# Batch-wise transposes of the first chunk, early state products and later transposes of the second chunk in a fused attention and MLP kernel

## The chip, the cores and the metric

The kernel runs on one core of a Trainium2 chip. The metric is the device time of one execution in microseconds; lower is better. Each number of the profile comes from one profiled execution.

The engines are PE (TensorE: matrix products and transposes), DVE (VectorE), ACT (ScalarE), POOL (GpSimd, which here also issues the loads that change the type) and SP (SyncE, which issues the other DMAs).

## What is computed

Two steps, the second on the result of the first. The first is linear attention with decay, for 4 batches, 8 heads, 768 positions and a head size of 64, in blocks:

```python
for b in range(nb):
    ...
    intra = np.einsum('bhic,bhjc->bhij', qb, kb) * Dmask[None]
    intra = np.einsum('bhij,bhjd->bhid', intra, vb)
    inter = np.einsum('bhid,bhde->bhie', qb * lam_pow[None], kv_state)
    out[:, :, sl] = intra + inter
    kb_dec = kb * rev_pow[None]
    kv_state = lam_block[None, :, None, None] * kv_state + np.einsum('bhsd,bhse->bhde', kb_dec, vb)
```

The second is an MLP on the 3072 x 512 result x, with w_in (512 x 2048) and w_out (2048 x 512):

```python
h = x @ w_in
s = np.sin(alpha * h)
g = h + s * s / (alpha + 1e-09)
return (g @ w_out).astype(np.float32)
```

## The kernel before

**Tiling.** The 768 positions are cut into six chunks of 128 (`t` or `g`). A chunk of the four batches gives 512 rows of x, which are one group of the MLP. A unit `u = 4 t + b` is one chunk of one batch with all eight heads. Batch 1 of chunk 0 is u = 1, chunk 1 is u = 4 to 7.

**Attention of one unit.** `transposes(u)` (L173) makes QT and KT: eight transposes on PE into one PSUM tile of 128 x 1024, one copy on ACT (L183). `scores(u)` (L196) makes eight products F_ps on PE and the masked STm on DVE (L209). `intra_mm` and `inter_mm` (L244, L254) add STm times v and the state kv times QT in O_ps, and `copy_x(u)` (L261) scales O_ps by Etab into the tile xt of the chunk, on DVE. For chunk 0 there is no state yet, and `first_out` (L345) does the two steps without it.

**State.** `decay_k(u)` (L166) scales k on POOL into kdec. `state_mm(us)` (L213) makes 16 products a unit pair on PE and copies the result into kvs (for chunk 0 a plain copy on DVE, L227). `state_put` and `state_decay` on POOL bring it into kv and prepare the next sum.

**MLP of one group.** Sixteen steps f. `hidden(g, f)` (L278) is four products of 128 x 512 on PE into hps, then Sin on ACT (s_sb, L286) and the square s (L289), on ACT or, for even f up to 6 in group 0, on DVE (L295). `finish` (L292) makes gall on DVE, which also frees the PSUM buffer of hps. `project` (L305) multiplies four of the sixteen gall slices with w_out, and a copy on ACT and a DMA on SP follow the last of them.

**What sets the order.** The order of every engine is written out by hand: instructions stand on an engine in the order in which the code issues them, and an engine takes them strictly in that order. The parts that matter here:

- *Loads.* k and q of batch 0 come over SP as kraw and qraw and are cast on DVE (L334, L341). All else comes over POOL: chunk 0 for batches 1 to 3 (and v of batch 0), then the small identity idf (16 x 16, two POOL instructions, L125 and L126), then four parts of w_in, k and q of chunk 1 for batches 0 and 1, the last part of w_in, four `decay_k`, and the rest of chunk 1. A load on POOL waits until the eighth load before it has landed. The decayed k of chunk 0 comes behind all of w_in.
- *The front.* L362 to L402 lay out PE's order until the first `hidden(0, 0)`: for batch 0 KT and QT apart, in half tiles of 128 x 512 (L363 to L370), then batch after batch, with `spin(n)` between. `spin(n)` (L356) is n matmuls on a constant tile; nobody reads their result. The text calls them fills. Among them is `a_ps` (L387), a transpose of alpha with the identity idf; `alpha_sb` and `r_sb` (L392, L394) are made from it on DVE.
- *Group 0.* `slots(0)` (L426) says what PE does behind which step f. Behind f = 3 and 6 stand the state products of chunk 0 (`part_k`), behind f = 7 and 8 the transposes of units 4 and 5, behind f = 12 those of unit 6, behind f = 13 the products of unit 5 and the transposes of unit 7. `feed(0)` (L452) says what POOL does ahead of which step. At the end of group 0 (L503 to L512) the last two units of chunk 1 are finished between parts of `project(0, ...)`. `hidden(1, 0)` follows; it needs xt of all of chunk 1.

Of the kernel before, what the change touches and what calls it, by code (L numbers as in the profile page):

```python
# [9 lines left out]
ACTF = mybir.ActivationFunctionType  # L10
FP32 = mybir.dt.float32
# [4 lines left out]
def kernel(  # L16
# [11 lines left out]
    nc = tc.nc  # L28
    P = nc.NUM_PARTITIONS

    B, H, S, D = q.shape
# [13 lines left out]
    consts = ctx.enter_context(tc.tile_pool(name="consts", bufs=1))  # L45
# [25 lines left out]
    qn, kn, vn = {}, {}, {}  # L71
    KQV = ((kn, k), (qn, q), (vn, v))

    def new_chunk(t):
        for d, nm in ((qn, "qn"), (kn, "kn"), (vn, "vn")):
            d[t] = qkvp.tile([P, B, H, D], BF16, name=nm)
# [8 lines left out]
    def load(t, i, b0, b1):  # L85
        dst, src = KQV[i]
        nc.gpsimd.dma_start(  # L87
            out=dst[t][:, b0:b1, :, :].rearrange("p b h e -> p (b h) e"),
            in_=src[b0:b1, :, t * T:(t + 1) * T, :].rearrange("b h p e -> p (b h) e"))

    def load_w_in(i):
        f0, f1 = W_IN[i]
        nc.gpsimd.dma_start(out=w_in_sb[i][:],  # L93
                            in_=moe_w_in[:, f0 * P:f1 * P].rearrange("(c p) g -> p c g", p=P))
# [29 lines left out]
    load(0, 2, B - 1, B)  # L124
    idf = consts.tile([NFC, NFC], FP32, name="idf")  # L125
    make_identity(nc, idf[:])  # L126
    for i in range(4):
        load_w_in(i)
    new_chunk(1)
    load(1, 0, 0, 2)  # L130
    load(1, 1, 0, 2)
    load_w_in(4)

    kv = [consts.tile([P, HP, 2, D], BF16, name=f"kv{b}") for b in range(B)]
    for b in range(B):
# [30 lines left out]
    def decay_k(u):  # L166
        t, b = divmod(u, B)
        if t < NT - 1:
            kdec = kdp.tile([P, H, D], BF16, name="kdec")
            nc.gpsimd.tensor_tensor(out=kdec[:], in0=kn[t][:, b, :, :], in1=head_bc(Rtok), op=ALU.mult)  # L170
            st[u]["kdec"] = kdec

    def transposes(u, tag="pqk"):  # L173
        t, b = divmod(u, B)
        QK_ps = psA.tile([P, 2, HP, T], BF16, name="QK_ps", tag=tag)
        for hp in range(HP):
            nc.tensor.transpose(out=QK_ps[:, 1, hp, :],
                                in_=kn[t][:, b, 2 * hp:2 * hp + 2, :], identity=iden[:])
        for hp in range(HP):
            nc.tensor.transpose(out=QK_ps[:, 0, hp, :],  # L180
                                in_=qn[t][:, b, 2 * hp:2 * hp + 2, :], identity=iden[:])
        QKT = qkp.tile([P, 2, HP, T], BF16, name="QKT")
        nc.scalar.copy(out=QKT[:], in_=QK_ps[:])  # L183
        st[u]["QT"], st[u]["KT"] = QKT[:, 0, :, :], QKT[:, 1, :, :]
# [11 lines left out]
    def scores(u, halves=1):  # L196
        QT, KT = st[u]["QT"], st[u]["KT"]
        F_ps = psA.tile([P, 2, HP, T], FP32, name="F_ps", tag="pf")
        for hp in range(HP):
            for hd in range(2):  # L200
                nc.tensor.matmul(out=F_ps[:, hd, hp, :],  # L201
                                 lhsT=KT[hd * D:(hd + 1) * D, hp, :],
                                 rhs=QT[hd * D:(hd + 1) * D, hp, :],
                                 start=True, stop=True)
        STm = work.tile([P, 2, HP, T], BF16, name="STm")
        n = HP // halves
        for s in range(halves):
            w = slice(s * n, (s + 1) * n)
            nc.vector.tensor_tensor(out=STm[:, :, w, :], in0=F_ps[:, :, w, :], in1=Cmask[:, :, w, :],  # L209
                                    op=ALU.mult)  # L210
        st[u]["STm"] = STm

    def state_mm(us, tag="pqk"):  # L213
        KVA_ps = psA.tile([P, 2, HP, D], FP32, name="KVA_ps", tag=tag)
        for n, u in enumerate(us):
            t, b = divmod(u, B)
            for hp in range(HP):
                for hd in range(2):
                    h = 2 * hp + hd
                    nc.tensor.matmul(out=KVA_ps[hd * D:(hd + 1) * D, n, hp, :],  # L220
                                     lhsT=st[u]["kdec"][:, h, :], rhs=vn[t][:, b, h, :],
                                     start=True, stop=True)
        for n, u in enumerate(us):
            t, b = divmod(u, B)
            kvs[u] = ksp.tile([P, HP, D], FP32, name="kvs")
            if t == 0:
                nc.vector.tensor_copy(out=kvs[u][:], in_=KVA_ps[:, n, :, :])  # L227
            else:
                nc.vector.tensor_tensor(out=kvs[u][:], in0=KVA_ps[:, n, :, :], in1=kvd[b][:], op=ALU.add)  # L229

# [101 lines left out]


    nc.vector.tensor_copy(out=kn[0][:, 0, :, :], in_=kraw[:])  # L334
    for u in range(B):
        decay_k(u)
    load(1, 2, 0, 2)
    for i in range(3):
        load(1, i, 2, 4)
# [5 lines left out]
    def first_out(u, tag, hps_=range(4)):  # L345
        O_ps = psA.tile([P, HP, T], FP32, name="O_ps", tag=tag)
        for hp in hps_:
            for hd in range(2):
                nc.tensor.matmul(out=O_ps[hd * D:(hd + 1) * D, hp, :],
                                 lhsT=vn[0][:, u, 2 * hp + hd, :], rhs=st[u]["STm"][:, hd, hp, :],  # L350
                                 start=True, stop=True, skip_group_check=True)
        w = slice(hps_[0], hps_[-1] + 1)
        nc.vector.tensor_tensor(out=xt[0][:, w, u * T:(u + 1) * T], in0=O_ps[:, w, :],
                                in1=Etab[:, w, :], op=ALU.mult)

    def spin(n, cols=512):  # L356

        ps = psA.tile([P, GRP], FP32, name="hps", tag="h0")
        for _ in range(n):
            nc.tensor.matmul(out=ps[:, 0:cols], lhsT=fill[:, 0:P], rhs=fill[:, 0:cols], start=True, stop=True)  # L360

    spin(9)  # L362
    for nm, src, tag in (("KT", kn, "pqk"), ("QT", qn, "ops")):  # L363
        X_ps = psA.tile([P, HP, T], BF16, name="X_ps", tag=tag)
        for hp in range(HP):
            nc.tensor.transpose(out=X_ps[:, hp, :], in_=src[0][:, 0, 2 * hp:2 * hp + 2, :], identity=iden[:])
        XT = qkp.tile([P, HP, T], BF16, name=nm + "0")
        nc.scalar.copy(out=XT[:], in_=X_ps[:])
        st[0][nm] = XT[:]
        spin(3)  # L370
    scores(0)
    spin(1)
    transposes(1, "pqk")
    for hp in range(HP):
        nc.scalar.activation(out=Etab[:, hp, :], in_=pos_row[:], func=ACTF.Exp, scale=ln_hd[:, hp:hp + 1])
    spin(2)
    transposes(2, "ops")
    warm = consts.tile([P, 1], FP32, name="warm")
    nc.scalar.activation(out=warm[:], in_=lnlam[:, 0:1], func=ACTF.Sin)
    spin(1)  # L380
    scores(1)
    spin(1)
    first_out(0, "po")
    spin(1)
    scores(2)
    a_ps = psA.tile([P, NFC], FP32, name="a_ps", tag="h2")
    nc.tensor.transpose(out=a_ps[:], in_=alpha_fp[:], identity=idf[:])  # L387
    transposes(3, "pqk")
    spin(2)
    first_out(1, "h1")  # L390
    alpha_sb = consts.tile([P, NFC], FP32, name="alpha_sb")
    nc.vector.tensor_copy(out=alpha_sb[:], in_=a_ps[:])  # L392
    r_sb = consts.tile([P, NFC], FP32, name="r_sb")
    nc.vector.reciprocal(out=r_sb[:], in_=alpha_sb[:])  # L394
    spin(2)
    scores(3, 2)
    spin(1)
    first_out(2, "po")
    spin(2)
    first_out(3, "h1", range(0, 2))  # L400
    first_out(3, "ops", range(2, 4))
    spin(3)  # L402


    def part_fo(uf, uo, tag=None):
# [20 lines left out]
    def slots(g):  # L426

        u = [B * (g + 1) + b for b in range(B)]
        T_, FO = transposes, part_fo
        if g == 0:  # L430
            return {3: [(part_k, (0, 1), "pf")], 6: [(part_k, (2, 3), "pf")],
                    7: [(T_, u[0])], 8: [(T_, u[1], "po")], 9: [(FO, u[0], None)],
                    11: [(FO, u[1], u[0]), (copy_x, u[0])], 12: [(T_, u[2])],
                    13: [(FO, None, u[1]), (T_, u[3], "ops"), (copy_x, u[1])], 14: [(FO, u[2], None)]}, {}
        if g == 1:
            return {4: [(part_k, (4, 5), h_tag(1, 5))], 6: [(part_k, (6, 7), h_tag(1, 7))],
                    8: [(FO, u[0], None)], 10: [(FO, u[1], u[0], h_tag(1, 11))],
                    12: [(FO, u[2], u[1], h_tag(1, 13))],
                    14: [(FO, u[3], u[2], h_tag(1, 15)), (copy_x, u[2])],
                    15: [(FO, None, u[3], h_tag(2, 0)), (copy_x, u[3])]}, {10: u[0], 12: u[1]}  # L440
        at = (3, 6, 9, 12, 14) if g == 2 else (1, 4, 7, 10, 13)
        tg = [h_tag(g, f + 1) if g < NT - 2 else None for f in at[1:]]
        return {at[0]: [(FO, u[0], None)], at[1]: [(FO, u[1], u[0], tg[0])], at[2]: [(FO, u[2], u[1], tg[1])],
                at[3]: [(FO, u[3], u[2], tg[2])], at[4]: [(FO, None, u[3], tg[3])]}, \
               {at[n + 1]: u[n] for n in range(4)}
# [98 lines left out]
```

## Time and profile before

| | |
|---|---|
| median of 3 runs | 219.26 us (218.94 to 219.39) |
| profiled execution | 219.22 us, of which the span from the first to the last instruction is 217.5 us |
| PE | 208.3 us busy (96%) |
| ACT | 147.2 us (68%) |
| DVE | 126.6 us (58%) |
| POOL | 94.3 us (43%) |
| chain that ended last | PE 78%, POOL 10%, DMA 5% |
| first `hidden` of group 0 starts | 18.48 us |
| last ACT instruction of group 0 ends | 42.17 us |
| first `hidden` of group 1 starts | 46.26 us |

In timeline lines the columns are start, length, engine, line, operation, out<-in with shapes, and how many instructions were merged. In brackets stands how long the engine had been idle, and what ended that. A busy PE in this profile is not PE at its peak, since the ends of matmuls are modelled. The landing time of a load is its issue time plus the time to landing that the table of DMA issues gives.

### The profile page before, as it was taken

Reading aid. Unit: us, or ns where it says so; the run is one execution under the profiler, and the core shown is the slowest. Engines: PE = TensorE matmul, PEld = TensorE weight load, DVE = VectorE, ACT = ScalarE, POOL = GpSimd, SP = SyncE. Lnnn points to the kernel's source line nnn. Section 1 sums busy time; section 2 is a strip of 40 time slices with the busy share of each in tenths; the row PEclk is TensorE's granted clock in tenths of the full one; section 3 lists DMA queues with packets and bytes.
Section 4 is the critical chain, followed back from the end, with each engine's and each line's share of the span. In section 5 each row is a group of like instructions: output and inputs, shape, how many; then the busy total and the mean of one; then the engine's idle time right before and its main releaser. Section 6 shows DMA issues by size and latency. Waiting matters only on the chain.

```text
span 217.5 us, 3864 instructions
## 1 busy us (share of the span) xinstructions
PE 208.3 (96%) x1504; PEld 99.6 (46%) x1504; DVE 126.6 (58%) x183; ACT 147.2 (68%) x234; POOL 94.3 (43%) x131
## 2 busy tenths in 40 slices
PE   7799986999999999999999999999999999999994
PEld 2354443544444544445454444444444444444453
DVE  4576977834656875567656777545767544444300
ACT  5573998728766648766667675777676779787521
POOL 7999999963899569052474611100000000000000
PEclk9999999999999999999999999999999999999999
DMA  5999999999999999929689990490110101111022
GB/s 102 150 158 198 176 167 184 208 175 154 197 176 136 177 148 139 189 46 135 143 101 124 166 119 29 116 128 21 75 50 3 48 0 48 51 50 48 0 101 96
DMA packets 99747, 24.65 MB, mean 113 GB/s; under 512 B 91904, under 2 KB 96784, under 8 KB 99728
## 3 DMA queue, kind: packets, MB, share of 16 engines
q0 software_dynamic: 76976, 13.37, 79.0%
q1 hardware_dynamic: 22752, 11.03, 23.6%
q8 instruction: 12, 0.20, 0.4%
q14 instruction: 7, 0.06, 0.1%
HBM read 27.28 MB, written 6.29 MB: 154 GB/s over the span
## 4 chain that ended last, share of the span: by engine, by line
PE 78%; POOL 10%; DMA 5%; ACT 2%; issue 2%; DVE 1%; POOLq 0%; ACTq 0%
PE ops L311 36%; PE hps L283 32%; DMA qn<-in_q_dram 5%; PE O_ps L257 3%; PE F_ps L201 2%; POOL vn L87 2%; PE O_ps L249 2%; POOL kdec L170 2%; POOL qn L87 2%; POOL w_in L93 2%; PE KVA_ps L220 2%; PE hps L325 2%; POOL kn L87 2%; ACT s_sb L286 1%; ACT s L289 1%
## 5 line engine op out<-in xcount | busy, mean ns | idle before, releaser
L296 DVE SCALAR_TENSOR_TENSOR gall<-s,r_sb,hps 128x512 bf16<-128x512 bf16 x96 | 71.2, 745 | 67.0 <-ACT s L289 66.7
L286 ACT ACTIVATE s_sb<-hps,alpha_sb 128x512 bf16<-128x512 f32 x96 | 65.8, 687 | 49.7 <-PE hps L283 49.7
L283 PE MATMUL hps<-xt,w_in 128*128 128x512 bf16 x384 | 97.6, 379 | 0.1
L311 PE MATMUL ops<-w_out,gall 128*128 128x512 bf16 x368 | 93.0, 379 | 0.0
L289 ACT ACTIVATE s<-s_sb 128x512 bf16<-128x512 bf16 x92 | 58.0, 630 | 3.0
L283 PEld LDWEIGHTS <-w_in 128*128 128x128 bf16 x384 | 36.9, 98 | 44.3 <-DVE kvs L229 0.9
L311 PEld LDWEIGHTS <-gall 128*128 128x128 bf16 x368 | 34.8, 98 | 38.3
L235 POOL CAST kv<-kvs 64x256 bf16<-64x256 f32 x40 | 16.0, 401 | 41.8 <-PE O_ps L257 36.8
L209 DVE TENSOR_TENSOR STm<-F_ps,Cmask 128x1024 bf16<-128x1024 f32 (+1 forms) x25 | 29.4, 1178 | 3.8 <-PE F_ps L201 3.1
L170 POOL TENSOR_TENSOR kdec<-kn,Rtok 128x512 bf16<-128x512 bf16 x20 | 20.9, 1065 | 2.8 <-DMA kn<-in_k_dram 2.5
L316 ACT COPY o_sb<-ops 128x512 f32<-128x512 f32 x23 | 13.2, 572 | 6.4 <-PE ops L311 6.4
L263 DVE TENSOR_TENSOR xt<-O_ps,Etab 128x512 bf16<-128x512 f32 x20 | 13.7, 684 | 1.7 <-PE O_ps L257 1.6
L87 POOL DMA_DIRECT2D vn<-in_v_dram x12 | 14.2, 1195 | 0.0
L87 POOL DMA_DIRECT2D kn<-in_k_dram x11 | 13.5, 1227 | 0.3 <-issue 0.3
L87 POOL DMA_DIRECT2D qn<-in_q_dram x11 | 13.3, 1206 | 0.0
L360 PE MATMUL hps<-fill 128*128 128x512 bf16 x31 | 10.8, 455 | 1.5 <-DVE fill L112 1.5
L241 POOL TENSOR_TENSOR kvd<-kvs,L 128x256 f32<-128x256 f32 x16 | 9.8, 615 | 1.0
L249 PE MATMUL O_ps<-STm,vn 128*64 128x128 bf16 x160 | 8.0, 222 | 1.1 <-DVE STm L209 0.6
L183 ACT COPY QKT<-QK_ps 128x1024 bf16<-128x1024 bf16 x7 | 7.0, 1002 | 2.0 <-PE QK_ps L180 1.9
L249 PEld LDWEIGHTS <-vn 128*64 128x64 bf16 x160 | 5.3, 110 | 4.5 <-issue 3.5
L220 PEld LDWEIGHTS <-kdec 128*64 128x64 bf16 x160 | 3.8, 111 | 6.8 <-issue 6.4
L201 PE MATMUL F_ps<-QT,KT 64*128 64x128 bf16 x136 | 6.8, 219 | 0.0
(61 smaller groups left out, 84.5 us busy)
## 6 DMA issues: line engine op xcount, KB each, us to landing
out_dram<-o_sb SPq DMA_DIRECT2D x23, 256.0 KB, 2.7
w_out<-in_moe_w_out_dram POOLq DMA_DIRECT2D x4, 512.0 KB, 14.0
w_in<-in_moe_w_in_dram POOLq DMA_DIRECT2D x3, 512.0 KB, 9.5
kn<-in_k_dram POOLq DMA_DIRECT2D x6, 256.0 KB, 10.9
qn<-in_q_dram POOLq DMA_DIRECT2D x6, 256.0 KB, 11.3
vn<-in_v_dram POOLq DMA_DIRECT2D x6, 256.0 KB, 11.3
kn<-in_k_dram POOLq DMA_DIRECT2D x2, 512.0 KB, 7.5
qn<-in_q_dram POOLq DMA_DIRECT2D x2, 512.0 KB, 8.5
```

The lines of the kernel that those rows point to most:

```text
L87: nc.gpsimd.dma_start(out=dst[t][:, b0:b1, :, :].rearrange("p b h e -> p (b h) e"), in_=src[b0:b1, :, t * T:(t + 1) * T, :].rearrange("b h ...
L170: nc.gpsimd.tensor_tensor(out=kdec[:], in0=kn[t][:, b, :, :], in1=head_bc(Rtok), op=ALU.mult)
L209: nc.vector.tensor_tensor(out=STm[:, :, w, :], in0=F_ps[:, :, w, :], in1=Cmask[:, :, w, :], op=ALU.mult)
L235: nc.gpsimd.tensor_copy(out=kv[b][s, :, hd, :], in_=kvs[u][s, :, :])
L249: nc.tensor.matmul(out=O_ps[hd * D:(hd + 1) * D, hp, :], lhsT=vn[t][:, b, 2 * hp + hd, :], rhs=st[u]["STm"][:, hd, hp, :], start=(hp == 0) ...
L263: nc.vector.tensor_tensor(out=xt[t][:, :, b * T:(b + 1) * T], in0=st[u]["O_ps"][:], in1=Etab[:], op=ALU.mult)
L283: nc.tensor.matmul(out=hps[:], lhsT=w_in_of[f][:, c, :], rhs=xt[g][:, c, :], start=(c == 0), stop=(c == NDC - 1))
L286: nc.scalar.activation(out=s_sb[:], in_=hps[:], func=ACTF.Sin, scale=alpha_sb[:, f:f + 1])
L289: nc.scalar.activation(out=s2[:], in_=s_sb[:], func=ACTF.Square)
L296: nc.vector.scalar_tensor_tensor(out=gall[g][:, f, :], in0=s2[:], scalar=r_sb[:, f:f + 1], in1=hps[:], op0=ALU.mult, op1=ALU.add)
L311: nc.tensor.matmul(out=ops[:], lhsT=gall[g][:, f, m * P:(m + 1) * P], rhs=w_out_sb[part][:, f % 4, :], start=(f == 0), stop=(f == NFC - 1))
L316: nc.scalar.copy(out=o_sb[:], in_=ops[:])
```

## The change

Five edits, all of them moves or splits; no product of the computation is added or left out.

- *POOL.* Only the first two parts of w_in are loaded ahead of the decays. `decay_k(0)` and `decay_k(1)` come next, then a part of w_in, `decay_k(2)` and `decay_k(3)`, and the remaining loads in their old order.
- *Transposes of chunk 0.* `half_T` makes KT or QT of one unit by itself: four transposes and a copy of 128 x 512. Units 0, 1 and 3 go through it, unit 2 keeps the whole `transposes`.
- *Order of the front.* PE's order is laid out anew. `a_ps` stands behind the transposes of unit 1 (it stood behind scores(2)), `scores(1)` and all that follows behind it. `first_out(1)` stands ahead of `scores(2)`. There are 28 fills where there were 31.
- *States of chunk 0.* The two `state_mm` stand in the front, ahead of `hidden(0, 0)`, and not behind f = 3 and 6. Their copies into kvs move from DVE to ACT.
- *Group 0.* The transposes of unit 6 move from behind f = 12 to behind f = 13 and the products of unit 5, next to those of unit 7. (The `copy_x` of unit 5 is issued ahead of them.)

```diff
-    for i in range(4):
-        load_w_in(i)
-    new_chunk(1)
-    load(1, 0, 0, 2)
-    load(1, 1, 0, 2)
-    load_w_in(4)
+    load_w_in(0)
+    load_w_in(1)
...
             if t == 0:
-                nc.vector.tensor_copy(out=kvs[u][:], in_=KVA_ps[:, n, :, :])
+                nc.scalar.copy(out=kvs[u][:], in_=KVA_ps[:, n, :, :])
...
-    for u in range(B):
-        decay_k(u)
+    decay_k(0)
+    decay_k(1)
+    load_w_in(2)
+    decay_k(2)
+    decay_k(3)
+    load_w_in(3)
+    new_chunk(1)
+    load(1, 0, 0, 2)
+    load(1, 1, 0, 2)
+    load_w_in(4)
     load(1, 2, 0, 2)
...
+    def half_T(u, nm, tag):
+        src = {"KT": kn, "QT": qn}[nm]
         X_ps = psA.tile([P, HP, T], BF16, name="X_ps", tag=tag)
         for hp in range(HP):
+            nc.tensor.transpose(out=X_ps[:, hp, :], in_=src[0][:, u, 2 * hp:2 * hp + 2, :], identity=iden[:])
         XT = qkp.tile([P, HP, T], BF16, name=nm + "0")
         nc.scalar.copy(out=XT[:], in_=X_ps[:])
+        st[u][nm] = XT[:]
```

The front in its new order, from the first fills to the first `hidden` (the activations of Etab and of the table warm-up are on ACT):

```python
    spin(9)
    half_T(0, "KT", "pqk")
    spin(3)
    half_T(0, "QT", "ops")
    spin(1)
    half_T(1, "KT", "pqk")
    spin(1)
    scores(0)
    half_T(1, "QT", "ops")
    ...
    nc.tensor.transpose(out=a_ps[:], in_=alpha_fp[:], identity=idf[:])
    ...
    spin(2)
    scores(1)
    spin(1)
    transposes(2, "pqk")
    ...
    spin(1)
    first_out(0, "po")
    spin(2)
    first_out(1, "h1")
    scores(2)
    half_T(3, "KT", "ops")
    spin(1)
    half_T(3, "QT", "pqk")
    spin(1)
    first_out(2, "po")
    scores(3, 2)
    state_mm((0, 1), "h2")
    spin(4)
    first_out(3, "h1", range(0, 2))
    first_out(3, "ops", range(2, 4))
    state_mm((2, 3), "pqk")
    spin(2)
```

And group 0:

```diff
-            return {3: [(part_k, (0, 1), "pf")], 6: [(part_k, (2, 3), "pf")],
-                    7: [(T_, u[0])], 8: [(T_, u[1], "po")], 9: [(FO, u[0], None)],
-                    11: [(FO, u[1], u[0]), (copy_x, u[0])], 12: [(T_, u[2])],
-                    13: [(FO, None, u[1]), (T_, u[3], "ops"), (copy_x, u[1])], 14: [(FO, u[2], None)]}, {}
+            return {7: [(T_, u[0])], 8: [(T_, u[1], "po")], 9: [(FO, u[0], None)],
+                    11: [(FO, u[1], u[0]), (copy_x, u[0])],
+                    13: [(FO, None, u[1]), (copy_x, u[1]), (T_, u[2]), (T_, u[3], "ops")],
+                    14: [(FO, u[2], None)]}, {}
```

## The prediction

> **What bounds the kernel now.** I read the busy time by stage first, because the page's shares (PE 96%, ACT 68%) mix stages with different limits. The columns are the stretch, its length, then for PE, PEld, DVE, ACT and POOL the busy time and the number of instructions, PEclk, DMA share, GB/s.
>
> ```profile
> 1.52:18.48 16.96, 15.28 (x128) 6.91 (x129) 11.30 (x22) 9.39 (x17) 16.78 (x24) 1.00 1.74 156
> 19.54:42.17 22.63, 20.36 (x194) 10.18 (x193) 18.66 (x28) 21.01 (x32) 22.13 (x28) 1.00 1.79 184
> 46.26:214.30 168.04, 167.99 (x1153) 80.22 (x1151) 92.80 (x128) 115.68 (x184) 49.75 (x69) 1.00 0.87 99
> ```
>
> From 46.26 us to the last matmul PE is busy 167.99 of 168.04 us. Nothing else limits that part, so whatever moves the first product of group 1 (46.26) moves the end by the same amount. In group 0 (19.54 to 42.17) ACT is busy 21.01 of 22.63 us, nearly as full as PE. Before 18.48 no engine of the path is full: that stage is a chain of hand-overs.
>
> Next, the timeline of ACT in group 0, to see where its idle time lies:
>
> ```profile
> 19.54 0.69 ACT L286 ACTIVATE s_sb<-hps,alpha_sb 128x512 bf16<-128x512 f32 x1 [4.20 <-PE hps L283]
> ...
> 26.54 0.69 ACT L286 ACTIVATE s_sb<-hps,alpha_sb 128x512 bf16<-128x512 f32 x1 [0.28 <-PE hps L283]
> ...
> 36.51 1.01 ACT L183 COPY QKT<-QK_ps 128x1024 bf16<-128x1024 bf16 x1 [0.61 <-PE QK_ps L180]
> ...
> 41.54 0.63 ACT L289 ACTIVATE s<-s_sb 128x512 bf16<-128x512 bf16 x1
> 47.33 0.69 ACT L286 ACTIVATE s_sb<-hps,alpha_sb 128x512 bf16<-128x512 f32 x1 [5.15 <-PE hps L283]
> ```
>
> The bracket is idle time before the instruction and who ended it. Between its first s_sb (19.54) and the end of the last s (42.17) ACT idles four times worth naming: 0.17 (at 20.41) and 0.18 (at 24.34), which the same timeline shows, 0.28 and 0.61 here. That is 1.24 us, so **ACT's own work with its pipeline gaps is 42.17 - 19.54 - 1.24 = 21.39 us**, and none of it is touched by the change. The 0.61 is the stall that the change aims at: PE waits for the late q of chunk 1 before its transposes.
>
> ```profile
> PE QK_ps L180 <- DMA qn<-in_q_dram: 1.2, 1, 1.2
> ```
>
> The chain of waits shows how ACT's end becomes PE's start: last s, last gall, then
>
> ```profile
> 42.87 1.22 DVE STm L209
> 44.09 0.61 DVE xt L263
> 44.70 0.04 issue
> 44.74 0.41 PE O_ps L249 x8
> ```
>
> and from there the last xt of chunk 1 and hidden(1,0) at 46.26. The program keeps this order after the change (DVE: gall 15, STm 7, xt 6, xt 7), so those 4.09 us stay.
>
> **The front.** Its timeline, PE, POOL and DVE in turn:
>
> ```profile
> 8.39 0.40 PE L201 MATMUL F_ps<-QT,KT 64*128 64x128 bf16 x8
> ...
> 11.46 0.40 PE L201 MATMUL F_ps<-QKT 64*128 64x128 bf16 x8
> ...
> 13.51 0.23 PE L387 MATMUL a_ps<-idf,alpha_fp 16*128 16x16 f32 x1
> ...
> 18.48 0.81 PE L283 MATMUL hps<-xt,w_in 128*128 128x512 bf16 x3
> ```
> ```profile
> 11.50 0.19 POOL masks.py:199 TENSOR_SCALAR_AFFINE_SELECT idf<-idf 16x16 f32<-16x16 f32 x1
> ```
> ```profile
> 11.90 1.23 DVE L209 TENSOR_TENSOR STm<-F_ps,Cmask 128x1024 bf16<-128x1024 f32 x1 [1.85 <-PE F_ps L201]
> ```
>
> The reader is to see that the small transpose of alpha (a_ps) needs idf, which POOL finishes only at 11.69, behind its ten loads of chunk 0. Before, PE comes to a_ps at 13.51 and doesn't notice. The change puts a_ps right behind the second transpose of batch 1, ahead of scores(1). POOL's order up to idf is the same, so **PE gets a new wait**, and everything of the front is queued behind it.
>
> **The front, step by step.** Unchanged up to the QT copy of batch 0 (7.75 to 8.34). kn of batch 1 landed at 1.44 + 5.8 = 7.2, so its transposes fit at 7.8 to 8.2 in the gap; scores(0) at 8.39 as before; qn of batch 1 landed at 2.48 + 5.7 = 8.2, its transposes run 8.7 to 9.1 (0.39 a group of four). PE then idles until 11.73: 2.6 us.
> - a_ps 0.17 to its successor; two fills to 12.35 (0.59 for two less 0.38 for one: 0.21 each); scores(1) 12.45 to 12.85, against 11.46. STm 1: 12.9 to 14.1.
> - One fill, transposes(2) 13.0 to 13.6, its copy 1.01 to 14.65, then the Sin table 1.28 and warm 0.20 to 16.15, and only then the two half copies of batch 3 (0.59 each) to 17.25.
> - first_out(1) waits for STm 1: 14.6 to 15.0; scores(2) to 15.35; DVE xt 0, xt 1 (0.68 each) to 15.75, STm 2 to 16.87.
> - first_out(2) 16.9 to 17.3, xt 2 17.4 to 18.05. It now stands ahead of STm 3 on DVE, so DVE idles 0.5 while PE works; scores(3) 17.3 to 17.7 (KT, QT ready 17.25).
> - STm 3 in halves 18.0 to 19.2; on PE state_mm(0,1) 0.44, four fills to 18.95, first_out(3) 19.0 and 19.25 to 19.55; last xt 20.1.
> - state_mm(2,3) 0.44 and two fills: **hidden(0,0) at 20.4 instead of 18.48: 1.9 us later.**
>
> Bounds: with DVE's pieces back to back behind STm 1, STm 3 ends at 18.6; half of first_out(3) 0.3, state_mm 0.44 and two fills 0.43 give 19.8 (1.3 later). With 0.05 more at each of eight hand-overs, 20.8 (2.3 later).
>
> **Group 0.** ACT starts 1.06 after hidden(0,0), as now: 21.46. Of the four gaps the first 0.17 stays; 0.18 and 0.28 (PE late by state_mm, 0.44 each at 22.02 and 25.09) go with the moved states; 0.61 goes, since qn landed at 24.34 + 11.7 = 36.04 and ACT comes to that copy only near 38.7 (its s of f 12 ended at 35.91, now 1.46 later, then s_sb and s of f 13, 1.32). ACT ends at 21.46 + 0.17 + 21.39 = 43.02, against 42.17. **Sum: 1.92 - 1.07 = +0.85 us**, through the same tail to hidden(1,0) at 47.1 and so to the end. The removed stall of PE (0.46 + 1.17) is worth only the 0.61 that ACT idled. Behind it another wait is near: hidden(0,13) and batch 5's products stand ahead of the transposes now, and the O_ps buffer that they need is freed by xt 4 at about 37.6 (s of f 10 at 33.43 + 1.46 = 34.9, then gall 0.75, STm 5 1.22, xt 4 0.68 on DVE); transposes(6) end near 38.65, just ahead of ACT. I put 0 to 0.2 there.
>
> **Edits at no cost, and their cover.** DVE loses four state copies of 0.42, ACT gets four of 0.37 (the row of the final 128x256 copies) at 18.1 to 20.7, in the stretch where it idled 4.20; they would cost only if hidden(0,0) came before 19.6. Splitting two copies into halves adds 2 x 0.59 - 1.01 = 0.16 each, in idle time too. POOL's four decays (4.29 together) move ahead of five loads: w_in of f 4 is issued at 15.35 instead of 13.22, f 8 at 18.2 instead of 13.96, kn of chunk 1 at 19.0 instead of 14.69, vn of chunk 1 at 22.15 instead of 21.98. The order of all loads is the same and the DMAs have a backlog (w_in of f 2 lands at 12.49 + 5.7 = 18.2, after f 4 is issued), so I cost it at 0; a dry queue could shift landings by at most some 0.3. f 4 is wanted at 20.4 + 4 x 0.86 = 23.9 and landed at 13.22 + 7.6 = 20.8, f 8 not before 28 and 13.96 + 9.5 = 23.5: covered. Decay 3 ends at 18.25, before state_mm(2,3) wants it at 19.45. SP's queue is untouched.
>
> **The clock.** PE's first nine fills are 0.43 apart, until 5.54, which is 4.0 us after the first; later ones are 0.21 apart. At the end the clock fell:
>
> ```profile
> 213.90:217.30 3.40, 0.35 (x4) 0.07 (x1) 0.00 (x0) 0.37 (x1) 0.00 (x0) 1.00 0.22 79
> 217.20:217.50 0.30, 0.00 (x0) 0.00 (x0) 0.00 (x0) 0.00 (x0) 0.00 (x0) 0.66 0.00 0
> ```
>
> PE was busy 0.35 of the 3.40 us before 217.3, then the clock was half (mean 0.66). A new idle stretch of 2.6 us leaves a stretch of that length up to 23% busy at the worst place, more where it falls otherwise: between the 11% that lost the clock and the 81% (2.75 of 3.41, from 5.67 to 9.08) that kept it. Cost: 0, or, if PE then needs 4.0 us at half speed again, at most 4.0 / 2 = 2.0, part of it in waits. I take 0, because 11% is the nearer row and 23% is twice that, and keep 1.5 as a case. The Trainium skill ("TensorE: Matmul & The Clock Gate", Part 1) says that the clock is halved after at least one idle window of about 3.4 us. By that rule 2.6 us of idling cost nothing and the sum stays +0.85; by a reading in which a thinly used window counts as idle it would be about +2.35.
>
> **Rivals.**
> 1. *The clock falls* in the new wait: hidden(0,0) near 21.9, 219.22 + 0.85 + 1.5 = 221.6. For: 23% is nearer to 11% than to 81%. Against: the stretch must lie just so. 18%.
> 2. *Faster:* PE catches up in the front's slack (it has 1.7 us of gaps there), and group 0 gives its 1.07 us. The earliest start is set by decay 3 (18.25) with state_mm(2,3) and two fills behind it: 19.05, 0.57 late, so 219.22 - 0.5 = 218.7. It decides where hidden(0,0) starts before 18.48 + 1.07 = 19.55. Against: STm 1 alone is 1.0 late, and DVE's order adds 0.5. 10%.
> 3. *It cancels:* hidden(0,0) near 19.6, or ACT has slack that I don't see: 219.3. 12%.
>
> **Numbers.** The forecast has 60%. The profiled execution took 219.22 us (span 217.5), within 0.04 of the median 219.26, so +0.85 gives 220.1. The range, 219.2 to 221.7, holds the forecast's bounds (+0.3 to +1.45), the cancelling case and most of the clock's; outside are the faster case and the worst of the clock. About 0.2%, or 0.44 us, is what a measurement of this kernel can tell from no change. Faster by more: 0.10; within: 0.15 (case 3 and the low end of the forecast); slower: 0.75.
>
> **What would show it.** In the profile after: a gap of 2.6 us on PE ahead of a_ps, ended by POOL idf; scores(1) near 12.45; hidden(0,0) near 20.4; no DMA wait ahead of transposes(6); ACT from 21.5 to 43.0 with less than 0.3 us idle; hidden(1,0) near 47.1. I am wrong if hidden(0,0) starts before 19.6, if ACT shows gaps in group 0, or if PEclk shows less than 9 in slices 3 and 4 (10.9 to 21.7 us).

## The result

The changed kernel took **221.61 us** (median of 11 runs, 220.09 to 222.74), the kernel before 219.26 (11 runs, 218.94 to 219.59): a ratio of 1.0108, 95% interval 1.0082 to 1.0133. It is slower, and its runs spread over 2.6 us where those of before spread over 0.65. The profiled execution happens to be one of the quickest: 220.11 us, span 218.4. So the profile shows only one part of the loss, and the spread holds the other.

**The profile after.** The timeline of PE in the front:

```profile
8.70 0.40 PE L372 MATMUL X_ps<-iden,qn 128*128 128x128 bf16 x4
11.71 0.23 PE L389 MATMUL a_ps<-idf,alpha_fp 16*128 16x16 f32 x1 [2.61 <-POOL idf masks.py:199]
...
12.41 0.40 PE L197 MATMUL F_ps<-QT,KT 64*128 64x128 bf16 x8
...
20.47 3.83 PE L279 MATMUL hps<-xt,w_in 128*128 128x512 bf16 x17
```

The new wait is there, 2.61 us, and hidden(0,0) starts at 20.47 instead of 18.48. The timeline of ACT in group 0:

```profile
21.53 0.69 ACT L282 ACTIVATE s_sb<-hps,alpha_sb 128x512 bf16<-128x512 f32 x1 [0.97 <-PE hps L279]
22.40 0.69 ACT L282 ACTIVATE s_sb<-hps,alpha_sb 128x512 bf16<-128x512 f32 x1 [0.18 <-PE hps L279]
...
42.32 0.63 ACT L285 ACTIVATE s<-s_sb 128x512 bf16<-128x512 bf16 x1
48.10 0.69 ACT L282 ACTIVATE s_sb<-hps,alpha_sb 128x512 bf16<-128x512 f32 x1 [5.15 <-PE hps L279]
```

The gaps of 0.18, 0.28 and 0.61 that the prediction aims at are gone (the 0.18 shown here is the first gap, 0.17 before, which was to stay). ACT starts 1.99 later (21.53 against 19.54), ends 0.78 later (42.95 against 42.17), and the end of the span is 0.9 later. Behind that PE is full again, as the busy times of the stage from hidden(1,0) on show (columns as in the prediction):

```profile
47.04:215.10 168.06, 166.90 (x1132) 80.24 (x1151) 92.93 (x128) 115.64 (x184) 49.49 (x69) 1.00 0.88 99
```

That is 0.9 of 2.35 us. The rest does not show in this execution, whose granted clock was 1.000. Each run also has its mean granted clock, and of the 11 only two have 1.000. These took 220.09 and 220.11, all others 221.18 or more, at clocks from 0.985 to 0.992.

### The profile page after: what moved, and what is told of

It is laid out like the page before. It is cut to its first block, busy times and chain, and to the rows that moved or that the text cites. A ratio compares the mean times of both kernels' runs of the same rounds, so it can differ in the third digit from the quotient of the medians.

```text
span 218.4 us, 3832 instructions
## 1 busy us (share of the span) xinstructions
PE 205.8 (94%) x1474; PEld 100.0 (46%) x1501; DVE 125.6 (58%) x179; ACT 148.3 (68%) x240; POOL 93.9 (43%) x131
## 4 chain that ended last, share of the span: by engine, by line
PE 79%; DVE 7%; ACT 6%; POOL 4%; issue 3%; ACTq 0%; POOLq 0%
PE ops L307 34%; PE hps L279 32%; DVE gall L292 3%; PE O_ps L253 3%; PE F_ps L197 3%; ACT s_sb L282 2%; PE O_ps L245 2%; DVE STm L205 2%; ACT s L285 2%; PE KVA_ps L216 2%; PE hps L321 2%; POOL vn L87 2%; POOL qn L87 1%; ACT QKT L179 1%; PE hps L365 1%
## 5 line engine op out<-in xcount | busy, mean ns | idle before, releaser
L279 PE MATMUL hps<-xt,w_in 128*128 128x512 bf16 x374 | 96.4, 379 | 0.8 <-DVE gall L292 0.2
L307 PE MATMUL ops<-w_out,gall 128*128 128x512 bf16 x353 | 90.8, 379 | 0.8
L205 DVE TENSOR_TENSOR STm<-F_ps,Cmask 128x1024 bf16<-128x1024 f32 (+1 forms) x25 | 29.4, 1180 | 2.6 <-PE F_ps L197 2.0
L365 PE MATMUL hps<-fill 128*128 128x512 bf16 x26 | 10.2, 491 | 1.6 <-DVE fill L112 1.5
L197 PE MATMUL F_ps<-QT,KT 64*128 64x128 bf16 x152 | 7.6, 219 | 0.0
L179 ACT COPY QKT<-QK_ps 128x1024 bf16<-128x1024 bf16 x5 | 4.9, 1005 | 2.8 <-PE QK_ps L176 2.7
L225 DVE TENSOR_TENSOR kvs<-KVA_ps,kvd 128x256 f32<-128x256 f32 x16 | 6.7, 422 | 0.1
```

The lines of the kernel that those rows point to most:

```text
L197: nc.tensor.matmul(out=F_ps[:, hd, hp, :], lhsT=KT[hd * D:(hd + 1) * D, hp, :], rhs=QT[hd * D:(hd + 1) * D, hp, :], start=True, stop=True)
L279: nc.tensor.matmul(out=hps[:], lhsT=w_in_of[f][:, c, :], rhs=xt[g][:, c, :], start=(c == 0), stop=(c == NDC - 1))
L307: nc.tensor.matmul(out=ops[:], lhsT=gall[g][:, f, m * P:(m + 1) * P], rhs=w_out_sb[part][:, f % 4, :], start=(f == 0), stop=(f == NFC - 1))
```

## The experiments

Two theories were put against each other. **The clock:** the rest of the loss is a fall of PE's clock behind the idle stretch ahead of a_ps. **The loads:** it is late landings, from POOL's new order. Ratios are to the kernel before, timed on the same chip as each experiment.

### 1. Fills in the wait

```diff
+    spin(12)
     a_ps = psA.tile([P, NFC], FP32, name="a_ps", tag="h2")
```

> The changed kernel with 12 more fills just ahead of a_ps (12 x 0.216 = 2.6 us), so that PE works while it has to wait for idf. The wait stays, the idle stretch goes. Theory (the clock falls behind the idle stretch in most executions): hidden(0,0) still near 20.4, all executions near 220.1 (219.8 to 220.4), the spread of the changed kernel (220.09 to 222.74) gone, clock 1.000 in every one. Rival (the spread comes from loads that land late, or from the order of the front): 221.6 and the same spread.

Measured: 220.49 us (12 runs, 220.08 to 221.39), ratio 1.006 (1.0039 to 1.008). In its profile the wait for idf is as long as before but filled, and hidden(0,0) starts at the same time:

```profile
11.70 0.23 PE L390 MATMUL a_ps<-idf,alpha_fp 16*128 16x16 f32 x1 [0.24 <-POOL idf masks.py:199]
...
20.47 2.75 PE L279 MATMUL hps<-xt,w_in 128*128 128x512 bf16 x12
```

No run had a clock below 0.998, and six of the twelve lie between 220.08 and 220.39. Work that nobody reads makes the kernel about 1.1 us quicker: the idle stretch was the cost, not only the wait. But the other six runs reach 221.39 at clocks of 0.998 to 1.000, so the expected end of the spread did not come. Late loads are the candidate for that rest; experiments 2, 4 and 5 bear on it.

### 2. The changed kernel again

Unchanged, to see its runs beside their clocks.

> The changed kernel once more, to see executions in which the clock fell. Theory: the time goes with the granted clock. Executions at 1.000 take 220.1, those with one stretch of half clock of about 3.4 us (mean clock 0.992) about 221.6, those with two (0.985) about 222.6; hidden(0,0) near 20.4 in the first and 22 to 23 in the others. Rival: late loads make the spread; then time and clock are not ordered alike.

Measured: 221.65 us (6 runs, 220.11 to 222.87), ratio 1.0106 (1.0072 to 1.0141). With the 11 runs above, by mean clock:

| mean clock | runs | us |
|---|---|---|
| 0.999 to 1.000 | 4 | 220.09, 220.11, 220.11, 220.87 |
| 0.989 to 0.992 | 8 | 221.18 to 221.83 |
| 0.985 | 5 | 222.49 to 222.87 |

Time goes with the clock from row to row: 1.1 to 1.7 us for the first step, some 1.0 for the second. (Not within a row: the two runs at 0.989, 221.18 and 221.19, are quicker than those at 0.992.) One stretch of 3.4 us at half clock in a span of 219.9 gives 1 - 0.5 x 3.4 / 219.9 = 0.992, two give 0.985. Thirteen of 17 runs lost the clock; of the 96 runs of the kernel before, timed here and beside the experiments, three have a clock below 0.995. No profile caught the changed kernel with a fallen clock, so where in it the clock falls is taken from experiments 1 and 3. The run at 220.87 is the one whose profile was taken. Its hidden(0,0) starts at 20.48, but q of chunk 1 comes late, and ACT has a gap that the first profile lacks. PE, then ACT:

```profile
20.48 7.07 PE L279 MATMUL hps<-xt,w_in 128*128 128x512 bf16 x32
...
29.43 0.40 PE L176 MATMUL QK_ps<-iden,qn 128*128 128x128 bf16 x4 [1.16 <-DMA qn<-in_q_dram]
```
```profile
29.86 1.01 ACT L179 COPY QKT<-QK_ps 128x1024 bf16<-128x1024 bf16 x1 [0.65 <-PE QK_ps L176]
```

### 3. The wait alone

The kernel before, with a_ps, alpha_sb and r_sb moved up:

```diff
     transposes(1, "pqk")
+    a_ps = psA.tile([P, NFC], FP32, name="a_ps", tag="h2")
+    nc.tensor.transpose(out=a_ps[:], in_=alpha_fp[:], identity=idf[:])
...
     transposes(2, "ops")
...
-    a_ps = psA.tile([P, NFC], FP32, name="a_ps", tag="h2")
-    nc.tensor.transpose(out=a_ps[:], in_=alpha_fp[:], identity=idf[:])
```

> The kernel before with only a_ps, alpha_sb and r_sb moved up, behind the transposes of batch 1. PE then idles about 2.1 us for idf. Theory: hidden(0,0) near 20.1 instead of 18.48, the gaps of group 0 take 0.6 to 0.9 of it back: 220.1 where the clock stays, up to 1.5 more where it falls; a clock below 0.995 in some executions. Rival (the wait is hidden by waits for q and v that were there already): 219.3.

Measured: 220.51 us (10 runs), ratio 1.0056 (1.0032 to 1.008). The runs fall in two groups: five at clock 1.000 with 219.90 to 220.14, five at 0.992 with 220.87 to 221.31. So the wait costs about 0.9, and the clock 1.2 where it falls; the theory holds. This profile caught a fall. PE's timeline, then the busy times of the 3.41 us before the fall, of those at half clock, and of those after:

```profile
11.94 0.23 PE L375 MATMUL a_ps<-idf,alpha_fp 16*128 16x16 f32 x1 [2.92 <-POOL idf masks.py:199]
...
13.68 0.63 PE L360 MATMUL hps<-fill 128*128 128x512 bf16 x1
...
15.81 0.39 PE L360 MATMUL hps<-fill 128*128 128x512 bf16 x1
```
```profile
8.84:12.25 3.41, 0.49 (x6) 0.25 (x4) 0.72 (x2) 2.18 (x5) 3.30 (x7) 1.00 2.19 140
12.25:15.66 3.41, 3.41 (x28) 1.84 (x26) 1.16 (x3) 1.72 (x2) 3.41 (x5) 0.50 1.87 152
15.66:19.07 3.41, 3.41 (x46) 1.71 (x44) 3.14 (x5) 1.79 (x3) 3.41 (x5) 1.00 1.26 178
```

The column PEclk reads 1.00, 0.50, 1.00. A fill takes 0.63 in the middle stretch and 0.39 after it. The fall came behind a stretch in which PE was busy 0.49 of 3.41 us (14%). The borders of these stretches are not chosen: in this trace the record of the granted clock begins at 5.42 us and reads full for 6.83 us, half for 3.41 and full for 204.80, which are 2, 1 and 60 times 3.413. The records of all twelve profiles fit such a grid, and they begin anywhere from 4.25 to 7.38 us, so the place of the borders differs from execution to execution.

### 4. a_ps behind scores(2)

The changed kernel without the wait:

```diff
     half_T(1, "QT", "ops")
...
-    a_ps = psA.tile([P, NFC], FP32, name="a_ps", tag="h2")
-    nc.tensor.transpose(out=a_ps[:], in_=alpha_fp[:], identity=idf[:])
...
     scores(2)
+    a_ps = psA.tile([P, NFC], FP32, name="a_ps", tag="h2")
+    nc.tensor.transpose(out=a_ps[:], in_=alpha_fp[:], identity=idf[:])
```

> The changed kernel with a_ps, alpha_sb and r_sb put back behind scores(2), where PE reaches idf when it is ready. Everything else of the change stays. Theory (the wait for idf is the whole loss): scores(1) near 10.1, hidden(0,0) near 19.1, set by decay 3 with state_mm(2,3) and two fills behind it, 0.6 later than before; group 0 gives back 1.07, so 218.8 (218.5 to 219.1) with no spread. Rival (the splits, the early states or DVE's order cost as much as the wait): 219.7 or more.

Measured: 220.45 us (12 runs, 219.14 to 221.81), ratio 1.0047 (1.0017 to 1.0077). The front did what was expected, scores(1) at 10.17 and hidden(0,0) at 19.04:

```profile
10.17 0.40 PE L197 MATMUL F_ps<-QT,KT 64*128 64x128 bf16 x8 [0.65 <-DVE STm L205]
...
19.04 3.61 PE L279 MATMUL hps<-xt,w_in 128*128 128x512 bf16 x16
```

The total did not, nor is the spread gone: two of the twelve runs have a clock of 0.992 (the other ten have a median of 220.30). In the profile the 1.4 us that the front gained are lost again in group 0. PE's timeline there, then ACT's:

```profile
23.18 3.63 PE L279 MATMUL hps<-xt,w_in 128*128 128x512 bf16 x15 [0.53 <-DMA w_in<-in_moe_w_in_dram]
27.66 0.40 PE L173 MATMUL QK_ps<-iden,kn 128*128 128x128 bf16 x4 [0.85 <-ACT s_sb L282]
29.07 0.40 PE L176 MATMUL QK_ps<-iden,qn 128*128 128x128 bf16 x4 [1.01 <-DMA qn<-in_q_dram]
```
```profile
29.50 1.01 ACT L179 COPY QKT<-QK_ps 128x1024 bf16<-128x1024 bf16 x1 [1.21 <-PE QK_ps L176]
```

Now PE waits for w_in of f 4 and for q of chunk 1. PE had that q at 26.81 in the profile before, and at 28.54 in the changed kernel, where the late start of group 0 hid it. Before, then after:

```profile
26.81 0.40 PE L180 MATMUL QK_ps<-iden,qn 128*128 128x128 bf16 x4
```
```profile
28.54 0.40 PE L176 MATMUL QK_ps<-iden,qn 128*128 128x128 bf16 x4 [0.77 <-DMA qn<-in_q_dram]
```

The number is the rival's (219.7 or more), but the waits that this profile shows in group 0 are for loads, which the rival does not name. The two theories of this section, the clock and the loads, are both right: there are two losses, and the first covers the second.

### 5. POOL's order alone

The kernel before, with the four decays between the loads as in the change (its diff of the loads and decays, nothing else).

> The kernel before with only POOL's order changed: the four decays stand between the loads of w_in as in the changed kernel. Theory A (the loads have a backlog, as the prediction put it): 219.2, q of chunk 1 for batch 0 and 1 lands near 26.8. Theory B (the queue runs dry while POOL decays, as the traces of the changed kernels suggest with 93 and 136 KB in two microseconds where 190 and 208 flowed before): that q lands near 28.4, ACT idles about 1 us ahead of the first QKT of group 0, part of it given back at the second wait, 219.7 to 220.2.

Measured: 220.21 us (12 runs, 219.62 to 221.57), ratio 1.0051 (1.0031 to 1.007); clock 0.997 or more in all. Theory B holds. What the DMAs moved in three stretches of 2 us (last column, GB/s), in the kernel before and here:

```profile
16.00:18.00 2.00, 2.00 (x21) 0.91 (x21) 2.00 (x5) 0.00 (x0) 2.00 (x3) 1.00 1.32 181
18.00:20.00 2.00, 1.94 (x10) 0.78 (x9) 0.58 (x2) 0.46 (x1) 2.00 (x3) 1.00 1.23 204
20.00:22.00 2.00, 2.00 (x10) 0.77 (x8) 1.70 (x3) 1.79 (x4) 2.00 (x3) 1.00 1.24 206
```
```profile
16.00:18.00 2.00, 2.00 (x22) 0.91 (x21) 2.00 (x5) 0.00 (x0) 1.98 (x3) 1.00 1.12 139
18.00:20.00 2.00, 1.94 (x10) 0.87 (x9) 0.45 (x2) 0.59 (x1) 2.00 (x4) 1.00 1.26 203
20.00:22.00 2.00, 2.00 (x16) 0.79 (x15) 1.51 (x3) 1.79 (x4) 2.00 (x3) 1.00 1.02 152
```

Twice, behind each pair of decays, the DMAs run short: 2 x (181 - 139) + 2 x (206 - 152) = 192 KB less, which is 0.94 us at 205 GB/s. That base is a high one: in the first stretch the six profiles with POOL's old order show 151 to 181, the five with the new one 98 to 146; in the third they show 199 to 208 and 114 to 176. So both drops are there in every profile, but 192 KB is more than a typical one. The first loads of chunk 1, k and q of batches 0 and 1, land at 26.7 and 28.2 instead of 25.3 and 26.7; k and q of batches 2 and 3 land at 34.4 and 36.4 against 34.5 and 36.0, so the lag has mostly gone by then. (That q lands at 26.7 to 28.5 in the six profiles with the old order and at 28.2 to 29.4 in the five with the new one: one pair of profiles does not give the size.) PE gets q at 28.23, and ACT waits:

```profile
28.66 1.01 ACT L179 COPY QKT<-QK_ps 128x1024 bf16<-128x1024 bf16 x1 [0.90 <-PE QK_ps L176]
```

By the timed runs POOL's order costs 1.0 us by itself (220.21 against 219.18).

### 6. What is left without the wait, POOL's order and the early states

The changed kernel with a_ps late, POOL's order as before, and the states behind f = 3 and 6 on DVE.

> The changed kernel with a_ps behind scores(2), POOL's order as before, and the states of chunk 0 behind f = 3 and 6 again with their copies on DVE. What is left of the change is the split transposes, the new order of the front and the late transposes(6). Theory (the wait for idf, the clock behind it and POOL's order are the whole loss): hidden(0,0) near 17.8, no clock below 0.995 except for a rare one, 218.7 (218.3 to 219.1), no slower than before. Rival (the front's new order itself costs): 219.5 or more.

Measured: 218.69 us (12 runs, 218.26 to 219.73), ratio 0.998 (0.9962 to 0.9999). All clocks are 0.998 or more. The split copies, the new order of the front and the late transposes of unit 6 are no loss, and together at most a small gain. The early states were taken out here together with POOL's order, and were not tried by themselves: from 0.998 to the 1.0047 of experiment 4 is 1.5 us, of which POOL's order alone gave 1.1, so they may have some 0.4, which is within the intervals. The front is quick enough now that the first w_in is what it waits for:

```profile
18.15 1.04 PE L283 MATMUL hps<-xt,w_in 128*128 128x512 bf16 x4 [0.68 <-DMA w_in<-in_moe_w_in_dram]
```

### 7. Group 0 alone

The kernel before with the last diff of the section on the change, but the states left behind f = 3 and 6.

> The kernel before with only the group 0 part of the move: transposes(6) behind f = 13 and the products of unit 5; states stay behind f = 3 and 6. Theory (ACT bounds group 0, and its 0.61 us of idle time at this place is all that the stall cost): ACT ends at 41.56, 219.22 - 0.6 = 218.65 (218.5 to 218.9). Rival (the stall of PE, 1.63 us, was the cost): 217.6. Second rival (the wait for xt 4 takes its place): 219.2.

Measured: 219.05 us (12 runs, 218.50 to 219.90), ratio 0.9995 (0.9975 to 1.0015). The expected 0.6 is not there, and the interval leaves room for at most 0.55. The profiled run, at 219.90 the slowest of the twelve, suggests why. The 0.61 ahead of unit 6 is gone in it (ACT's copies of units 6 and 7 start at 38.45 without a gap), but the first wait for q, at unit 4, was longer:

```profile
29.00 1.01 ACT L183 COPY QKT<-QK_ps 128x1024 bf16<-128x1024 bf16 x1 [0.87 <-PE QK_ps L180]
```

In the profile of before the first wait cost ACT nothing and the second 0.61. The second rival, whose number (219.2) is the nearest, is not seen: PE does wait 0.71 us for xt at 37.22, but ACT has no gap behind it. That late landings change places with each other from run to run in this way is argued from these two profiles, not shown for all runs.

### 8. Two squares less on ACT

```diff
     def on_act(g, f):
-        return f % 2 == 1 or f > 7 if g == 0 else True
+        return f % 2 == 1 or f > 11 if g == 0 else True
```

on top of experiment 7.

> As the group 0 part alone, and the squares of f = 8 and f = 10 in group 0 on DVE (0.42 each) instead of ACT (0.63 each). Theory (ACT bounds group 0): up to 1.26 less on ACT, part of which goes into waiting for transposes(6), whose q lands at 36.04: 218.0 (217.5 to 218.3). Rival (PE or DVE bounds group 0): the same as the group 0 part alone, 218.65, or slower.

Measured: 218.36 us (12 runs, 218.00 to 219.16), ratio 0.9966 (0.9947 to 0.9985), 0.7 us below experiment 7 and just above the range expected. That fits ACT as the bound of group 0, and this version beats both kernels.

### 9. Two attempts on top of that

k and q of chunk 1 for batches 0 and 1 ahead of w_in of f 8 to 11:

```diff
-    for i in range(4):
+    for i in range(3):
         load_w_in(i)
     new_chunk(1)
     load(1, 0, 0, 2)
     load(1, 1, 0, 2)
+    load_w_in(3)
     load_w_in(4)
```

> As the group 0 part with two squares on DVE, and k and q of chunk 1 for batches 0 and 1 loaded ahead of w_in of f 8 to 11 (which lands near 23.5 and is wanted near 27). Theory (what is left of ACT's idle time in group 0 is the wait for that q ahead of transposes(4)): q lands 2.6 us sooner, no wait ahead of transposes(4), 0.3 to 0.8 less than without: 217.8 (217.4 to 218.2). Rival (w_in of f 8 then lands too late, or the wait moves on to the later q): 218.4 or more.

Measured: 218.38 us (12 runs, 217.84 to 218.86), ratio 0.9955 (0.9933 to 0.9977), no different from 218.36. The rival holds: the wait moved on, to w_in, w_out and the later q. PE's waits, in total, times, longest:

```profile
PE ops L312 <- DMA w_out<-in_moe_w_out_dram: 1.0, 2, 0.6
PE hps L284 <- DMA w_in<-in_moe_w_in_dram: 0.9, 1, 0.9
...
PE QK_ps L181 <- DMA qn<-in_q_dram: 0.5, 1, 0.5
```

And the state products of chunk 0 behind f = 8 and 10 (with state_put and a load of w_out moved behind them on POOL):

```diff
-            return {3: [(part_k, (0, 1), "pf")], 6: [(part_k, (2, 3), "pf")],
-                    7: [(T_, u[0])], 8: [(T_, u[1], "po")], 9: [(FO, u[0], None)],
+            return {7: [(T_, u[0])], 8: [(T_, u[1], "po"), (part_k, (0, 1), "pf")], 9: [(FO, u[0], None)],
+                    10: [(part_k, (2, 3), "pqk")],
```

> As the group 0 part with two squares on DVE, and the state products of chunk 0 behind f = 8 and f = 10 instead of f = 3 and f = 6, where PE is ahead of ACT (their copies stay on DVE; state_put and one load of w_out follow on POOL). Theory (ACT's gaps of 0.18 and 0.28 come from the state products): 0.3 to 0.5 less than without, 217.9. Rival (PE or a late load binds there, so that the gaps return at the transposes): 218.4.

Measured: 219.95 us (12 runs, 219.10 to 221.91), ratio 1.0042 (1.0018 to 1.0066), 1.6 slower than experiment 8. Both expectations fail. PE reached the wait for k and q of chunk 1 sooner and idled there (0.71 and 1.04 us), and in three of the twelve runs the clock fell, now in the midst of group 0. From its profile, the stretch before the fall and the one at half clock:

```profile
24.95:28.36 3.41, 1.65 (x14) 0.76 (x12) 3.14 (x5) 2.18 (x5) 3.41 (x5) 1.00 1.74 189
28.36:31.77 3.41, 3.41 (x30) 1.88 (x28) 0.68 (x3) 2.59 (x3) 0.93 (x2) 0.50 2.26 161
```

Its runs at full clock are slower too (219.10 to 220.33). Which of its moves costs that stays open.

## Why the prediction was right or wrong

- **The new wait and the front: right.** Predicted 2.6 us ahead of a_ps, scores(1) at 12.45, hidden(0,0) at 20.4; measured 2.61, 12.41, 20.47.
- **Group 0 and the sum of +0.85: right for the runs at full clock in which q comes no later than in the profile.** ACT from 21.53 to 42.95 (predicted 21.5 to 43.0), gaps 0.18 and 0.08, span +0.9, and 220.09 to 220.11 where 220.1 was predicted (three runs of 17; a fourth at full clock took 220.87). The O_ps buffer as the next wait is in the chain of waits after, just ahead of the transposes of unit 6:

```profile
36.65 0.61 DVE xt L259
37.26 0.04 issue
37.30 0.41 PE O_ps L245 x8
```

- **The clock: this step failed, and it decided the median.** "I take 0, because 11% is the nearer row and 23% is twice that." The reason given speaks for a fall, not for 0. The fall was a rival with 18%; it came in 13 of 17 runs and costs 1.1 to 1.7 us for the first stretch at half clock, so that the median is the rival's 221.6 and not the forecast's 220.1. That 221.61 lies within the stated range, 0.09 under its upper end, is owed to that rival: the range was drawn to hold most of its case. Two rows bound what a stretch of 3.41 us may lose: 1.65 busy (48%, experiment 9) lost the clock, and in the profile before, in its wait for the late q, 1.78 (52%) kept it:

```profile
32.98:36.39 3.41, 1.78 (x17) 0.88 (x15) 2.93 (x4) 2.86 (x5) 3.31 (x4) 1.00 2.05 177
```

  In the changed kernel's profile the wait lay across the border of two stretches, 2.08 and 2.05 busy (61% and 60%), and the clock stayed:

```profile
6.93:10.35 3.42, 2.08 (x24) 1.14 (x22) 2.66 (x3) 2.29 (x6) 3.42 (x5) 1.00 2.38 148
10.35:13.76 3.41, 2.05 (x23) 1.12 (x25) 1.34 (x3) 0.69 (x3) 3.29 (x7) 1.00 2.61 144
```

  The twelve profiles agree with these bounds: on the grid of each, every stretch in which PE was busy less than half was followed by half clock, and every one of 52% or more by the full clock. The 52% stretch stands in the profile of before, so the prediction could have had it. It took 81% as the nearest row on the other side instead. With 48% and 52% as bounds the odds come out as an estimate: if a grid of 3.41 us is moved over the changed kernel's profile, its least busy stretch ahead of group 1 lies at 48% or less for about 73% of the places of the border and below 52% for about 80%; 13 of 17 is 76%. (For experiment 3 the same gives 83 to 90%, but only five of ten runs fell, so the estimate is rough.) The Trainium skill ("TensorE: Matmul & The Clock Gate", Part 1) asks for at least one idle window of about 3.4 us before the clock is halved. The length of the window agrees (3.41 us at half clock). What counts as idle does not: a window 48% busy was enough here, and the measurement decides.
- **The loads at "0", with "at most some 0.3": wrong in size, hidden in the forecast.** The argument was that the next load is issued before the last one lands. That was so in experiment 5 too (w_in of f 4 issued at 15.21, the part ahead of it landed at 19.8), and the DMAs ran short all the same. That a load has to be issued before the last one's data has flowed, which is sooner than its landing, is the likely reason; it was not tried. By itself POOL's order costs 1.0 (experiment 5). In the changed kernel the late start of group 0 covers it, though barely: PE has q at 28.54 and ACT's copy starts at 29.10 without a gap, while in the run of 220.87 it waits 0.65. The prediction named a cover for w_in, none for this q. So that 220.1 came out to 0.01 in the quickest runs is in part luck.
- **The stall taken away at 0.61: not seen in the time** where it was tried alone (experiment 7), though the gap itself is gone there.
- **The faster rival** (hidden(0,0) at 19.05 gives 218.7): the front came out so, at 19.04, but the time did not (220.45), since the rival too left out the late loads.

The ratios lay the loss out: 0.998 without the wait, POOL's order and the early states (experiment 6); 1.0047 with POOL's order and the early states (4); 1.006 with the wait as well, if it is filled (1); 1.0106 with the idle stretch (2). The wait itself adds next to nothing to the late loads (0.0013, within the intervals). The clock adds 0.0046, which is 1.0 us.

## What to carry to other kernels

An instruction moved up in an in-order engine needs all its operands followed to their producers, a small constant too: idf was the last thing that POOL made in its preamble. A wait of PE is priced twice, as time and as a loss of the clock, and for the second the rows to look for are the least busy stretches that kept the clock. Two delays in parallel hide each other in a profile: taking away the one that shows (220.45, experiment 4) gained no more than filling it did (220.49, experiment 1). Only with the other gone too did the time fall, to 218.69 (experiment 6).

## What was not expected of the hardware

- The clock fell on stretches that were half used (48%), not only on idle ones, and came back after one stretch of 3.41 us in both profiles that caught a fall (the runs at a mean of 0.985 fit two stretches). Whether a wait of 2 to 3 us costs it depends on where the borders of these stretches lie: 2.92 us within one stretch lost it (experiment 3), 2.61 us across a border kept it. By this and by late loads, runs of the same changed kernel lie up to 2.8 us apart.
- Landing times differ between runs of the same loads: PE had q of chunk 1 at 28.54 and 29.43 in two profiles of the changed kernel, while hidden(0,0) started at 20.47 and 20.48 in both. With POOL's old order it landed anywhere from 26.7 to 28.5 in six profiles. What makes the difference was not tried.
